# Block sums of the first products' weights: from pass 1 to pass 2

## The chip, the cores and the metric

The kernel runs on one core of a Trainium2 chip. The metric is the device time of one execution, in microseconds; the time of a kernel is the median of its runs.

## The reference

Attention with a compressive memory, followed by two feed-forward networks on the same 2304 tokens (4 batches of 576, model width 512):

```python
def _moe_ref(x, w_gate, w_val, w_out):
    g = x @ w_gate
    silu = g * (1.0 / (1.0 + np.exp(-g)))
    val = x @ w_val
    return (silu * val @ w_out).astype(np.float32)
...
def _moe2_ref(x, w_in, w_out):
    h = x @ w_in
    g = h * (1.0 / (1.0 + np.exp(-1.702 * h)))
    return (g @ w_out).astype(np.float32)
...
    x = np.ascontiguousarray(attn_out.transpose(0, 2, 1, 3)).reshape(B * S, H * D)
    x = _moe_ref(x=x, **moe_kwargs)
    return _moe2_ref(x=x, **moe2_kwargs)
```

The width between is 1536 in the first network (layer one below) and 2048 in the second (layer two). The weights come in 64-bit floats. The products are made to nearly full single precision: an operand is split into a high half, rounded to the type that the matmul reads (fp32r), and a low half, the rest, and a product is high x high + high x low + low x high.

## The kernel before

Activations lie transposed, model width on partitions, tokens on columns. Work goes in two passes over the tokens. Both are laid out by a planner written in the kernel: every step is an entry in `ops` with its engine, an assumed duration, a key (a due time; the lowest key that is ready goes first), what it waits for, and which ring of buffers it takes or gives back. `schedule` plays the entries through and returns one list; `pinned` emits them in that order, with every instruction tied behind the one before it on its engine, so that an engine works in the order of the plan.

Pass 1 takes the first 1024 tokens through both layers with ordinary products (line 89, tile `m`), and makes the attention of all tokens beside that. The weights are 68 chunks of 128 x 512 (`order`), each group of layer one being 8 chunks of its input weights and 4 of its output weights, each group of layer two 4 and 4. A chunk i is loaded by SyncE (`load_w`, L121), decoded to single precision by ScalarE (L140, L141), VectorE (L144, L146, L147) and GpSimd (L150) into a tile `wa`, and split by ScalarE (`spl0`, L161) and GpSimd (`spl1`, L164) into `wp`. There are three `wa`; one is free again when all readers are done.

Pass 2 takes the other 1280 tokens. It uses a scheme of Strassen's kind (Winograd's form) on 2 x 2 blocks: seven products in place of eight, on sums of weight blocks and of activation blocks. A pair of chunks (i even, i + 1) holds four quarters of 128 x 256. Of a pair's seven weight operands two are in the split `wp` (tile `da`), one in another part of `wp` (`dz`), and four are plain sums and differences of the quarters, which have to be split anew. What pass 2 needs is written to DRAM in pass 1 (`keep`, L177 to L187), ten blocks of 256 columns for each pair, in `kept`.

A product whose input is the layer's input is called a first product (`first(i)` is true; `P` in the plan), one whose input is the hidden activations a second product (`Q`). There are 20 pairs of the first kind (12 in layer one, 8 in layer two) and 14 of the second. Before the change the two kinds differ:

- For first products, pass 1 makes the four sums: `add_up` (L170, L171, L174, L175), four GpSimd instructions for each pair into the tile `sums`, after the pair's second chunk is split. They are written to `kept[:, 6:10]` in one transfer.
- For second products, the raw quarters are written (two transfers for each pair), and pass 2 makes the sums in place, by `add` (L1018), four GpSimd instructions for each pair.

In pass 2, SyncE fetches the four blocks (`raw`, L1005; two buffers) once both the last chunk of pass 1 is kept and the buffer is free. ScalarE makes the high half of each (`wh`, L1026), GpSimd the low half (`wl`, L1029), into a ring of six tiles `wb`, and TensorE multiplies (line 89, tile `c`). VectorE evicts and combines products (L1078, L1091, L1151, which read one operand from PSUM, or for L1091 also both from SBUF), makes the sums of activation blocks (L1113, `t1` to `t4`) and most of their low halves (L1134); GpSimd makes some of these low halves (L1134), and the multiplication by the gate (L1095). Two groups are interleaved, and units of layer two's first group two by two.

In the plan, the sums of pass 1 hold a place behind the split (`need + 5.0`), the in-place additions of pass 2 one right ahead of the first split of their quarters (`key - 1.0`).

Of the kernel before, what the change touches and what calls it, by code (L numbers as in the profile page):

```python
# [35 lines left out]
def tile_attention_moe_moe(  # L36
# [75 lines left out]
    def first(i):  # L112
        return layer(i)[1] < layer(i)[2]

    kept = {i: dram.tile([128, 10, 256], F32, name=f"w{i}") for i in range(0, NCK, 2)}
    bits, raws, parts, sums, stages = {}, {}, {}, {}, {}
# [49 lines left out]
    def add_up(i, x):  # L166
        a1, a2 = (raws[n].rearrange("p (a n) -> p a n", a=2) for n in (i - 1, i))
        if x == 0:
            m = sums[i] = d2.tile([128, 4, 256], F32, tag="sums", name="sums", bufs=1)
            nc.gpsimd.tensor_add(m[:, 2], a2[:, 0], a2[:, 1])  # L170
            nc.gpsimd.tensor_sub(m[:, 0], m[:, 2], a1[:, 0])  # L171
        else:
            m = sums[i]
            nc.gpsimd.tensor_sub(m[:, 1], a1[:, 0], a2[:, 0])  # L174
            nc.gpsimd.tensor_sub(m[:, 3], a1[:, 1], m[:, 0])  # L175

    def keep(i):  # L177
        odd, to = i % 2, kept[i - i % 2]
        w = f(parts[i])
        if odd:  # L180
            nc.sync.dma_start(out=to[:, 4:6], in_=w[:, :, 256:512])
        else:
            nc.sync.dma_start(out=to[:, 0:4], in_=w)
        if not first(i):
            nc.sync.dma_start(out=to[:, 6 + 2 * odd:8 + 2 * odd], in_=raws[i].rearrange("p (a n) -> p a n", a=2))
        elif odd:
            nc.sync.dma_start(out=to[:, 6:10], in_=sums.pop(i))  # L187
# [393 lines left out]
    def decode_ops(ops, i, use, split=True, decode=True):  # L581
# [11 lines left out]
        _, at_, ins, _ = layer(i)  # L593
        odd = i % 2
        if at_ >= ins:
            ops["keep", i] = "SP", 0.8 if odd else 1.2, need + 2.0, (("spl1", i),), (), (("wa", ("dec0", i)),)
            return
        if odd:
            for x in range(2):
                ops["sum", i, x] = "Pool", 1.75, need + 5.0, (("spl1", i),) if x == 0 else (("sum", i, 0),), \  # L600
                    ("sums",) if x == 0 else (), tuple(("wa", ("dec0", n)) for n in (i - 1, i)) if x else ()
        ops["keep", i] = "SP", 1.2 if odd else 0.8, need + 6.0, (("sum", i, 1) if odd else ("spl1", i),), (), (
            (("sums", ("sum", i, 0)),) if odd else ())
# [143 lines left out]
    def plan_three(ops, t0, ready, gets):  # L747
# [25 lines left out]
        for m, (i, j) in enumerate(flat):  # L773
            part = "da" if j < 2 else "raw" if j < 6 else "dz"
            key = keys[m] - (WB if part == "raw" else 0.0)
            new = seq[m][0] == "P"
            if (part, i) not in ops:
                ops[part, i] = "SP", 0.55 if part == "dz" else 1.1, key - (RAW if part == "raw" else DIR), (
                    ("seam", 1), *gets), (part,), ()
                if part == "raw" and not new:  # L780
# [546 lines left out]
```

## Time and profile before

| | us |
|---|---|
| median of 3 runs | 1019.97 (1019.64 to 1020.27) |
| the profiled execution | 1020.71 |
| its span, first to last instruction | 1018.9 |
| TensorE busy | 991.2 |
| VectorE busy | 838.0 |
| ScalarE busy | 562.8 |
| GpSimd busy | 696.8 |

The busy time of TensorE is from matmuls whose ends are modelled, so that a busy TensorE may still hide short waits. The granted clock of TensorE was at its full 2.4 GHz in nearly all of the span (mean 0.995). Times in the traces below are counted from the first instruction; pass 1 ends and pass 2 begins near 585 us, and layer two of pass 2 takes over from layer one around 777 to 832 us.

### The profile page before, as it was taken

Reading aid. Unit: us, or ns where it says so; the run is one execution under the profiler, and the core shown is the slowest. Engines: PE = TensorE matmul, PEld = TensorE weight load, DVE = VectorE, ACT = ScalarE, POOL = GpSimd, SP = SyncE. Lnnn points to the kernel's source line nnn. Section 1 sums busy time; section 2 is a strip of 40 time slices with the busy share of each in tenths; the row PEclk is TensorE's granted clock in tenths of the full one; section 3 lists DMA queues with packets and bytes.
Section 4 is the critical chain, followed back from the end, with each engine's and each line's share of the span. In section 5 each row is a group of like instructions: output and inputs, shape, how many; then the busy total and the mean of one; then the engine's idle time right before and its main releaser. Section 6 shows DMA issues by size and latency. Waiting matters only on the chain.

```text
span 1018.9 us, 16779 instructions
## 1 busy us (share of the span) xinstructions
PE 991.2 (97%) x5959; PEld 854.7 (84%) x5959; DVE 838.0 (82%) x1163; ACT 562.8 (55%) x1129; POOL 696.8 (68%) x703
## 2 busy tenths in 40 slices
PE   7998999999999999999999999999999899999997
PEld 4665777777777777777888899999999889999997
DVE  8998589789779889767868957747858999798988
ACT  6887575766465657675645534534324357454541
POOL 7887778997779685856656447748748646756564
PEclk9998999999999999999999999999999999999999
DMA  5353376757547555635575553333333242433322
GB/s 167 109 185 113 118 243 209 248 193 237 210 165 229 206 170 191 222 137 185 186 240 186 206 179 111 100 108 105 114 94 105 83 124 77 132 102 105 111 67 104
DMA packets 63300, 157.34 MB, mean 154 GB/s; under 512 B 8944, under 2 KB 18160, under 8 KB 63216
## 3 DMA queue, kind: packets, MB, share of 16 engines
q1 hardware_dynamic: 63072, 156.26, 46.7%
q8 instruction: 47, 0.77, 0.3%
q14 instruction: 37, 0.30, 0.1%
q10 hardware_dynamic: 144, 0.00, 0.0%
HBM read 104.34 MB, written 51.90 MB: 153 GB/s over the span
## 4 chain that ended last, share of the span: by engine, by line
PE 79%; DVE 17%; issue 1%; DMA 1%; ACT 1%; POOL 0%; SPq 0%; ACTq 0%; DVEq 0%
PE c L89 36%; PE m L89 31%; PE o L89 5%; PE s L89 3%; PE tp L363 2%; DVE nm L312 2%; DVE hl L968 1%; DVE phi L256 1%; DVE s L310 1%; DVE tl L1134 1%; DVE t L1113 1%; DVE acc L1151 1%; DVE wa L146 1%; DVE acc L1113 1%; DVE wa L147 1%
## 5 line engine op out<-in xcount | busy, mean ns | idle before, releaser
L89 PE MATMUL m<-xh,wp 128*128 128x512 f32 x640 | 210.0, 398 | 0.0
L1029 POOL TENSOR_TENSOR wb<-raw,wb 128x256 fp32r<-128x256 f32 x136 | 123.5, 919 | 86.9 <-ACT wb L1026 84.2
L89 PE MATMUL m<-hh,wp 128*128 128x512 f32 x448 | 148.0, 399 | 0.8 <-POOL wp L164 0.7
L89 PEld LDWEIGHTS m<-xh,wp 128*128 128x128 f32 x640 | 120.2, 188 | 32.9 <-issue 5.1
L150 POOL TENSOR_TENSOR wa<-wa,wr 128x512 uint32<-128x512 uint32 x68 | 99.0, 1456 | 62.8 <-DVE wa L147 51.2
L89 PE MATMUL m<-xl,wp 128*128 128x512 f32 x320 | 124.8, 390 | 0.0
L164 POOL TENSOR_TENSOR wp<-wa,wp 128x512 fp32r<-128x512 f32 x68 | 94.9, 1396 | 40.8 <-ACT wp L161 32.4
L1078 DVE TENSOR_TENSOR t<-t,c 128x640 f32<-128x640 f32 x100 | 81.4, 816 | 45.1 <-PE c L89 43.5
L1026 ACT CAST wb<-raw 128x256 fp32r<-128x256 f32 x136 | 53.2, 405 | 108.4 <-PE c L89 95.0
L89 PEld LDWEIGHTS m<-hh,wp 128*128 128x128 f32 x448 | 83.9, 188 | 23.7 <-issue 3.8
L1129 ACT CAST f<-t 128x640 fp32r<-128x640 f32 x98 | 69.4, 726 | 59.4 <-DVE t L1113 32.1
L89 PE MATMUL c<-f,wb 128*128 128x320 f32 x672 | 101.3, 309 | 0.3 <-DVE f L1134 0.3
L89 PEld LDWEIGHTS c<-f,wb 128*128 128x128 f32 x672 | 99.2, 188 | 0.5 <-DVE f L1134 0.5
L351 POOL TENSOR_SCALAR p<-p,sm 128x256 f32<-128x256 f32 (+3 forms) x128 | 78.5, 629 | 19.6 <-DVE sm L343 9.4
L89 PE MATMUL m<-hl,wp 128*128 128x512 f32 x224 | 87.5, 391 | 0.8 <-DVE hl L968 0.8
L1134 DVE TENSOR_TENSOR f<-t,f 128x640 fp32r<-128x640 f32 x70 | 76.5, 1096 | 10.1 <-ACT f L1129 9.8
L326 ACT ACTIVATE p<-s,nm 128x256 f32<-128x256 f32 (+3 forms) x128 | 66.1, 530 | 29.4 <-DVE nm L312 24.4
L1134 POOL TENSOR_TENSOR f<-t,f 128x640 fp32r<-128x640 f32 x28 | 50.4, 1801 | 39.9 <-ACT f L1129 39.8
L1113 DVE TENSOR_TENSOR t<-t,t 128x640 f32<-128x640 f32 x64 | 73.2, 1150 | 1.7 <-POOL t L1095 1.0
L89 PEld LDWEIGHTS m<-xl,wp 128*128 128x128 f32 x320 | 60.2, 188 | 11.6
L161 ACT CAST wp<-wa 128x512 fp32r<-128x512 f32 x68 | 42.3, 621 | 50.0 <-POOL wa L150 19.8
L147 DVE SCALAR_TENSOR_TENSOR wa<-w,wa 128x512 uint32<-128x512 uint32 x68 | 65.7, 965 | 2.3
(138 smaller groups left out, 2422.2 us busy)
## 6 DMA issues: line engine op xcount, KB each, us to landing
w<-w SPq DMA_DIRECT2D x40, 512.0 KB, 3.9
w<-wp SPq DMA_DIRECT2D x34, 512.0 KB, 2.9
raw<-w SPq DMA_DIRECT2D x34, 512.0 KB, 3.6
da<-w SPq DMA_DIRECT2D x34, 512.0 KB, 4.2
w<-wo SPq DMA_DIRECT2D x28, 512.0 KB, 4.0
w<-sums SPq DMA_DIRECT2D x20, 512.0 KB, 2.9
qk<-qk SPq DMA_DIRECT2D x32, 288.0 KB, 3.8
w<-wp SPq DMA_DIRECT2D x34, 256.0 KB, 2.6
```

Source lines behind the costliest of these rows:

```text
L89: nc.tensor.matmul(o, w, x, start=start, stop=stop, skip_group_check=more)
L147: nc.vector.scalar_tensor_tensor(au, top, 0xC0000000, au, op0=ALU.bitwise_and, op1=ALU.bitwise_or)
L150: nc.gpsimd.tensor_tensor(au, au, r, op=ALU.add)
L164: nc.gpsimd.tensor_sub(parts[i][:, 1], raws[i], f(parts[i][:, 0]))
L326: nc.scalar.activation(p[:, j, c:c + n], s[:, j, c:c + n], AF.Exp, bias=nm[:, x, j:j + 1], accum_out=sm[:, x, j:j + 1])
L351: nc.gpsimd.tensor_scalar(p[:, j, c:c + n], p[:, j, c:c + n], sm[:, x, j:j + 1], 1.0, op0=ALU.mult, op1=ALU.mult)
L1026: nc.scalar.copy(wb[:, 0], weight(m))
L1029: nc.gpsimd.tensor_sub(WBS[m][:, 1], weight(m), f(WBS[m][:, 0]))
L1078: nc.vector.tensor_add(wide_(t), wide_(TT[(a, *U)]), pc("P", *U, j))
L1113: nc.vector.tensor_sub(t, block(G, a, kd), block(G, b, kd))
L1129: nc.scalar.copy(form(G, F, kd)[0], block(G, SRC[F], kd))
L1134: e.tensor_sub(l, block(G, SRC[F], kd), f(h))
```

## The change

The sums for first products are no longer made in pass 1. `add_up`, its two entries of the plan for each pair and the tile `sums` go. `keep` writes the raw quarters of every chunk, and every pair's quarters are summed in pass 2 by `add`, as those of second products are: the entries `add` are made for all 34 pairs, `wh` waits for the fourth, and `weight` picks the block in the order that `add` leaves. `keep` has the same place in the plan (`need + 2.0`) for every chunk, and a `wa` is given back by it. `wl`, `raw`, the rings and the keys of all else stay.

```diff
--- before.py
+++ after.py
@@ -109,11 +109,8 @@
     def layer(i):
         return (0, i % 12, 8, i // 12) if i < 36 else (1, (i - 36) % 8, 4, (i - 36) // 8)
 
-    def first(i):
-        return layer(i)[1] < layer(i)[2]
-
     kept = {i: dram.tile([128, 10, 256], F32, name=f"w{i}") for i in range(0, NCK, 2)}
-    bits, raws, parts, sums, stages = {}, {}, {}, {}, {}
+    bits, raws, parts, stages = {}, {}, {}, {}
 
     def load_w(i):
         if wide:
@@ -163,17 +160,6 @@
     def spl1(i):
         nc.gpsimd.tensor_sub(parts[i][:, 1], raws[i], f(parts[i][:, 0]))
 
-    def add_up(i, x):
-        a1, a2 = (raws[n].rearrange("p (a n) -> p a n", a=2) for n in (i - 1, i))
-        if x == 0:
-            m = sums[i] = d2.tile([128, 4, 256], F32, tag="sums", name="sums", bufs=1)
-            nc.gpsimd.tensor_add(m[:, 2], a2[:, 0], a2[:, 1])
-            nc.gpsimd.tensor_sub(m[:, 0], m[:, 2], a1[:, 0])
-        else:
-            m = sums[i]
-            nc.gpsimd.tensor_sub(m[:, 1], a1[:, 0], a2[:, 0])
-            nc.gpsimd.tensor_sub(m[:, 3], a1[:, 1], m[:, 0])
-
     def keep(i):
         odd, to = i % 2, kept[i - i % 2]
         w = f(parts[i])
@@ -181,10 +167,7 @@
             nc.sync.dma_start(out=to[:, 4:6], in_=w[:, :, 256:512])
         else:
             nc.sync.dma_start(out=to[:, 0:4], in_=w)
-        if not first(i):
-            nc.sync.dma_start(out=to[:, 6 + 2 * odd:8 + 2 * odd], in_=raws[i].rearrange("p (a n) -> p a n", a=2))
-        elif odd:
-            nc.sync.dma_start(out=to[:, 6:10], in_=sums.pop(i))
+        nc.sync.dma_start(out=to[:, 6 + 2 * odd:8 + 2 * odd], in_=raws[i].rearrange("p (a n) -> p a n", a=2))
 
     BLOCKS = (((1, 0), (0, 256)), ((2, 0),), ((3, 0),), ())
     NP = B * HP
@@ -590,17 +573,7 @@
             return
         ops["spl0", i] = "Act", 0.63, need, (("dec2", i),), ("wp",), ()
         ops["spl1", i] = "Pool", 1.42, need, (("spl0", i),), (), ()
-        _, at_, ins, _ = layer(i)
-        odd = i % 2
-        if at_ >= ins:
-            ops["keep", i] = "SP", 0.8 if odd else 1.2, need + 2.0, (("spl1", i),), (), (("wa", ("dec0", i)),)
-            return
-        if odd:
-            for x in range(2):
-                ops["sum", i, x] = "Pool", 1.75, need + 5.0, (("spl1", i),) if x == 0 else (("sum", i, 0),), \
-                    ("sums",) if x == 0 else (), tuple(("wa", ("dec0", n)) for n in (i - 1, i)) if x else ()
-        ops["keep", i] = "SP", 1.2 if odd else 0.8, need + 6.0, (("sum", i, 1) if odd else ("spl1", i),), (), (
-            (("sums", ("sum", i, 0)),) if odd else ())
+        ops["keep", i] = "SP", 0.8 if i % 2 else 1.2, need + 2.0, (("spl1", i),), (), (("wa", ("dec0", i)),)
 
     def unit_ops(ops, i, c, key, ends, bank, lead=2.0):
 
@@ -773,16 +746,15 @@
         for m, (i, j) in enumerate(flat):
             part = "da" if j < 2 else "raw" if j < 6 else "dz"
             key = keys[m] - (WB if part == "raw" else 0.0)
-            new = seq[m][0] == "P"
             if (part, i) not in ops:
                 ops[part, i] = "SP", 0.55 if part == "dz" else 1.1, key - (RAW if part == "raw" else DIR), (
                     ("seam", 1), *gets), (part,), ()
-                if part == "raw" and not new:
+                if part == "raw":
                     for x in range(4):
                         ops["add", i, x] = "Pool", 0.7, key - 1.0, (("add", i, x - 1) if x else ("raw", i),), (), ()
             if part == "raw":
                 ops["wh", m] = "Act", 0.32, key, (
-                    ("raw", i) if new else ("add", i, 3), *([("wh", wh)] if wh is not None else [])), ("wb",), ()
+                    ("add", i, 3), *([("wh", wh)] if wh is not None else [])), ("wb",), ()
                 ops["wl", m] = "Pool", 0.7, key, (("wh", m),), (), (("raw", ("raw", i)),) if ends[i, "raw"] == m else ()
                 wh = m
         start = {}
@@ -1019,7 +991,7 @@
 
     def weight(m):
         i, j = flat[m]
-        return RAWS[i][:, j - 2 if first(i) else (0, 2, 3, 1)[j - 2]]
+        return RAWS[i][:, (0, 2, 3, 1)[j - 2]]
 
     def wh(m):
         wb = WBS[m] = cb.tile([128, 2, 256], F32R, tag="wb", name="wb")
@@ -1210,10 +1182,10 @@
     emit = attention(att)
     emit.update(
         w=load_w, dec0=lambda i: dec(i, 0), dec1=lambda i: dec(i, 1), dec2=lambda i: dec(i, 2), spl0=spl0, spl1=spl1,
-        sum=add_up, keep=keep, pe=pe, tanh=tanh, gate=gate1, val=val, hh=hh, hl=hl, acc=acc_in, out=out_to, y_hi=y_hi,
+        keep=keep, pe=pe, tanh=tanh, gate=gate1, val=val, hh=hh, hl=hl, acc=acc_in, out=out_to, y_hi=y_hi,
         y_lo=y_lo)
     for n, size in {"qk": 2, "nq": 2, "v": 2, "qt": 2, "e": 2, "ph": 2, "p": 4, "pt": 1, "st": 1, "zb": 1, "sc": 3,
-                    "big": 3, "wa": 3, "wr": 2, "sums": 1, "wp": 4, "u": 3, "h": 4, "m": 4}.items():
+                    "big": 3, "wa": 3, "wr": 2, "wp": 4, "u": 3, "h": 4, "m": 4}.items():
         at["fifo"][n] = size, []
     at["slots"]["ps"] = [0.0] * 4
     ops = plan_one()
```

## Rows read from the trace of the kernel before

**Rows 1.** Busy time of each engine over the whole span, the page's part 1.

```profile
PE 991.2 (97%) x5959; PEld 854.7 (84%) x5959; DVE 838.0 (82%) x1163; ACT 562.8 (55%) x1129; POOL 696.8 (68%) x703
```

**Rows 2.** By stage: length, then busy us of PE, PEld, DVE, ACT, POOL.

```profile
150.00:200.00 50.00, 47.94 (x248) 35.95 (x247) 43.16 (x62) 31.21 (x63) 44.03 (x41) 1.00 0.72 227
...
200.00:550.00 350.00, 350.00 (x1794) 275.22 (x1793) 282.24 (x420) 211.50 (x423) 251.88 (x243) 1.00 0.59 200
581.00:777.00 196.00, 195.02 (x1321) 194.09 (x1320) 134.36 (x146) 77.01 (x144) 128.17 (x120) 1.00 0.38 121
777.00:832.00 55.00, 48.79 (x319) 46.56 (x318) 54.62 (x64) 26.87 (x48) 30.86 (x26) 1.00 0.34 100
832.00:1010.00 178.00, 177.98 (x1213) 177.98 (x1214) 161.83 (x182) 87.98 (x155) 112.26 (x104) 1.00 0.30 95
```

**Rows 3.** Groups by line, sums of pass 1: busy us, mean ns, idle before.

```profile
L171 POOL TENSOR_TENSOR sums<-sums,wa 128x256 f32<-128x256 f32 x20 | 16.9, 844 | 1.6
L170 POOL TENSOR_TENSOR sums<-wa 128x256 f32<-128x256 f32 x20 | 16.8, 840 | 0.0
...
L174 POOL TENSOR_TENSOR sums<-wa 128x256 f32<-128x256 f32 x20 | 16.2, 812 | 0.0
L175 POOL TENSOR_TENSOR sums<-wa,sums 128x256 f32<-128x256 f32 x20 | 16.2, 811 | 0.0
```

**Rows 4.** Waits, whole span: who waited for whom, us, times, longest.

```profile
ACT wa L140 <- POOL sums L174: 4.5, 2, 2.5
...
ACT wa L140 <- DMA w<-wa: 4.2, 3, 2.5
```

**Rows 5.** Waits from 120 to 205 us.

```profile
PEld m L89 <- POOL wp L164: 1.6, 2, 0.8
```

**Rows 6.** Timeline, VectorE and GpSimd around 158 us: start, us, what.

```profile
156.91 1.78 DVE L147 SCALAR_TENSOR_TENSOR wa<-w,wa 128x512 uint32<-128x512 uint32 x1
...
158.10 1.19 POOL L170 TENSOR_TENSOR sums<-wa 128x256 f32<-128x256 f32 x1
...
161.45 1.75 POOL L150 TENSOR_TENSOR wa<-wa,wr 128x512 uint32<-128x512 uint32 x1
```

**Rows 7.** Tile raw: duration ns min/median/max, first and last start.

```profile
L1018 POOL TENSOR_TENSOR raw<-raw x56: 730/834/1393, 624.6 to 981.0; 128x256 f32<-128x256 f32 x56
...
DMA to landing us min/median/max: 3.3/3.6/6.9
```

**Rows 8.** Timeline, start of pass 2: SyncE, GpSimd, TensorE.

```profile
576.75 0.44 SPq L1005 DMA_DIRECT2D raw<-w  x1
...
581.72 4.68 POOL L1029 TENSOR_TENSOR wb<-raw,wb 128x256 fp32r<-128x256 f32 x4 [7.68 <-ACT wb L1026]
...
586.62 0.46 PE L89 MATMUL c<-th,wb 128*128 128x320 f32 x2
```

**Rows 9.** Timeline, seam of the layers: SyncE, VectorE, GpSimd.

```profile
783.67 8.55 SPq L1005 DMA_DIRECT2D raw<-w  x2
...
792.64 0.81 DVE L1113 TENSOR_TENSOR t<-t,t 128x640 f32<-128x640 f32 x1
...
798.67 1.35 DVE L1113 TENSOR_TENSOR t<-t,t 128x640 f32<-128x640 f32 x1
...
798.00 1.34 POOL L1029 TENSOR_TENSOR wb<-raw,wb 128x256 fp32r<-128x256 f32 x1 [0.84 <-POOL wb L1029]
...
800.91 1.99 POOL L1134 TENSOR_TENSOR f<-t,f 128x640 fp32r<-128x640 f32 x1 [1.57 <-ACT f L1129]
```

**Rows 10.** Groups by line, VectorE's evictions, 787 to 802 us.

```profile
L1151 DVE SCALAR_TENSOR_TENSOR acc<-c,acc 128x640 f32<-128x640 f32 x6 | 4.7, 810 | 0.0
...
L1151 DVE SCALAR_TENSOR_TENSOR csum<-c,csum 128x640 f32<-128x640 f32 x3 | 2.4, 809 | 0.0
```

**Rows 11.** Timeline, VectorE's waits for a product in layer two, first and last.

```profile
881.67 0.82 DVE L1078 TENSOR_TENSOR t<-t,c 128x640 f32<-128x640 f32 x1 [2.76 <-PE c L89]
...
980.21 0.82 DVE L1078 TENSOR_TENSOR t<-t,c 128x640 f32<-128x640 f32 x1 [1.37 <-PE c L89]
```

## The prediction

> **What bounds the kernel now.** The first view is the busy table of the page [rows 1]: TensorE is busy for 97% of the span, VectorE for 82%, GpSimd for 68%. An average like that names TensorE, but the change moves GpSimd work from one half of the kernel to the other, so the second view is the table of busy time by stage [rows 2]. The reader is to look for the stages in which TensorE is not full, since only there can a microsecond be won, and for the engine that is full in its place. From 200 to 550 us (the body of pass 1) TensorE is busy for 350.00 of 350 us. From 150 to 200 us it is busy for 47.94 of 50, and GpSimd, at 44.03, is busier than VectorE. From 581 to 777 us (layer one of pass 2) TensorE has 195.02 of 196. From 777 to 832 us, the seam between the layers of pass 2, it has 48.79 of 55 and VectorE has 54.62: VectorE is the bound there, and 6.2 us of TensorE are lost. From 832 to 1010 us TensorE is full again (177.98 of 178), with VectorE close behind at 161.83. So GpSimd bounds no long stage. It matters where it delays VectorE, and where its place in a chain decides when TensorE gets an operand.
>
> **Removed from pass 1.** 20 pairs of weight chunks lose four GpSimd instructions each, 80 in all; their four groups are busy for 16.8 + 16.9 + 16.2 + 16.2 = 66.1 us [rows 3]. In the 350 full microseconds this is worth nothing: TensorE's own work covers it, and without it GpSimd would idle more. In the stage that is not full it has a price. There the sums of one pair begin at 158.10, the next chunk's last decode instruction follows them at 161.45, while VectorE had finished the step before it at 156.91 + 1.78 = 158.69 [rows 6]. The sums kept that chunk back by 161.45 - 158.69 = 2.8 us. What the chunk feeds is late for TensorE by less: in 120 to 205 us TensorE waited for the split weights 1.6 us in two waits, 0.8 each [rows 5]. At most the whole idle of the stage, 50 - 47.94 = 2.1 us, comes back [rows 2]; at least nothing, because the VectorE steps of the following chunks are then next and are not shortened much. I take -1.0, between one such wait and both.
>
> **Moved in pass 1.** The first products' chunks now go to DRAM as raw quarters, 40 transfers of 256 KB in place of 20 of 512 KB, so bytes stay as they are and SyncE issues 20 more. The buffer of a raw chunk (three of them) was free when the sums had read it; now it is free when the transfer has landed. Twice in the run ScalarE waited for sums to free such a buffer, 4.5 us together, and three times for a transfer of a raw chunk, 4.2 us [rows 4]. The second kind is there today for 28 chunks and will be for 68, so by proportion 4.2 x 68 / 28 = 10.2 us: 6.0 more, against 4.5 less. That net 1.5 us falls on ScalarE, which is 55% busy [rows 1], and what is queued behind the waiting instruction there are the next tanh, split and exponent steps. I cost it at nothing, with +1.5 as its bad end; the good end, the 4.5 alone, lies within the 2.1 already counted.
>
> **Added to pass 2.** Each of the 20 first-product pairs gets four in-place additions on GpSimd between the landing of its quarters and their split. The second products have them today: 56 instructions, at least 0.730, median 0.834, at most 1.393 us [rows 7]. 80 of them are 66.7 us at the median. They fall into four places.
>
> At the start of pass 2 the first quarters are fetched at 576.75 [rows 8] and land some 3.6 us later [rows 7], near 580.4. Four low halves of the split then take 4.68 us, 1.17 each, beside VectorE's work, the first starting at 581.72; the first product that uses one starts at 586.62 [rows 8]. With four additions ahead, at 0.73 to 1.17 each, the first split ends 2.9 to 4.7 us later than 581.72 + 1.17 = 582.9, at 585.8 to 587.6. The cover ends at 586.62, so this costs 0 to 1.0 us. I take +0.4. TensorE is the only one to pay here, and everything after is shifted by it.
>
> In the rest of layer one, 12 pairs make 48 additions, 40.0 us at the median and 66.9 at the slowest. GpSimd is busy for 128.17 of 196 us [rows 2] and would reach 168 to 195. VectorE at 134.36 has room for being slowed. TensorE's cover is the ring of six split blocks. I take 0, with +1.5 as the bad end, since GpSimd works in the order of the plan and the multiplications by the gate stand in the same queue.
>
> At the seam VectorE has no idle time. The quarters for the first two units of layer two are fetched there, by two issues from 783.67 to 792.2 [rows 9], so eight additions run between about 787 and 802, on GpSimd's idle gaps of that stretch. What they cost is what they do to VectorE. A subtraction with both operands in SBUF takes two thirds more beside GpSimd: the one at 792.64, with GpSimd idle, took 0.81 us, the one at 798.67, beside the split that GpSimd began at 798.00, took 1.35 [rows 9]. The difference is 0.54 us. From 787 to 802 us 9 of VectorE's 20 instructions are evictions that read one operand from PSUM [rows 10]; about half have both in SBUF. So 8 x 0.54 / 2 = 2.2 us, at least 0, at most 8 x 0.54 = 4.3. Besides, the GpSimd split at 800.91 [rows 9] feeds a product that TensorE waits for; an addition that starts just before it pushes it by one instruction, 0.73 us, at most two (2 x 1.39). I take 2.2 + 0.7 = +2.9, with 0 and 4.3 + 2.8 = 7.1 as the ends.
>
> The contention is the one place where a rule may be weighed. The Trainium skill, SBUF — State Buffer, sections Who interferes with whom and Summary: rules for kernel authors, says that a VectorE instruction with two SBUF inputs contends with a GpSimd instruction that reads SBUF, and that the second of them to issue is blocked until the first has finished. The rows show a slowing by 0.54 us, less than a whole addition of 0.73; by the rule the seam would cost 8 x 0.73 / 2 = 2.9 instead of 2.2, and the sum below would be 0.7 us higher.
>
> After the seam, 24 additions come in three clusters of eight or fewer. VectorE is 91% busy, but catches up with TensorE once per group of units: at 881.67 it had waited 2.76 us for a product, at 980.21 still 1.37, three such places in all [rows 11]. A cluster slows it by 8 x 0.54 / 2 = 2.2 us, which these waits take up for the most part. I take +0.5 for the whole stage, from 0 to 6 (three clusters with every addition on a two-operand instruction, 3 x (4.3 - 1.37) = 8.8, less what the buffers between VectorE and TensorE hold). Nothing moves at the very end, where no first product is left.
>
> **The sum.** -1.0 + 0.4 + 0 + 2.9 + 0.5 = +2.8 us. It is made against the profiled execution, 1020.71 us with a span of 1018.9; that lies 0.74 above the median of the timed runs, 1019.97. Carried to the median: 1022.8 us, 0.27% slower. About 0.2%, 2.0 us, is what a measurement of this kernel can tell from no change.
>
> **The rivals.** First, no change: the eight additions at the seam meet VectorE mostly while it reads PSUM, and the split at 800.91 keeps its place. Then the seam costs 0.5 instead of 2.9 and the sum is +0.4: 1020.4 us. For it speaks that GpSimd has 55 - 30.86 = 24 us idle in that stage; against it, that the quarters land in the part where its queue is denser.
>
> Second, faster: the stage from 150 to 200 us is bound by the queue of GpSimd more than the waits say. Once the sums are out, the whole 2.1 us idle comes back, and the same again out of waits that the modelled end of a matmul hides, while the additions of pass 2 are free as in the first rival but for the start: -4.2 + 0.4 + 0.5 = -3.3, 1016.7 us. It decides if TensorE's gaps between 140 and 180 us vanish. Against it: TensorE's waits for split weights are 1.6 us there [rows 5], and VectorE's steps, which stay, feed the same chunks.
>
> Third, much slower: after the seam VectorE's slack (1.37 us at the smallest place) is less than what a cluster of eight additions takes from it, so every group of units ends with TensorE waiting, about 2 us in each of three groups on top of the forecast: 1022.8 + 6 - 0.5 = 1028.3 us. For it speaks the 91%; against it, that the catch-up of today is there in every group [rows 11].
>
> **How the numbers follow.** The forecast has 0.47, no change 0.26, faster 0.12, much slower 0.15. The forecast's own range is 1021.0 to 1026 (seam from 1.1 to 6), so that a tenth of its chance counts as no change. Slower by over 0.2%: 0.42 + 0.15 = 0.57; within: 0.26 + 0.05 = 0.31; faster: 0.12. The range that leaves out no more than two in ten reaches from below the first rival into part of the second, and nearly to the third: 1018.4 to 1027.8.
>
> **What would show it.** In the profile after: no group of sums, and 136 additions where 56 were. TensorE still full from 200 to 550 us and its busy time in 150 to 200 us up by about 1 us. The first product on a split block at most 1 us later against the start of pass 2. The seam stretch longer by about 3 us, with VectorE full in it and more of its two-operand instructions near 1.35 than near 0.81. In layer two, TensorE full, and VectorE's waits for products shorter than 2.76 and 1.37, but there. The prediction is wrong if the seam keeps its length, if TensorE shows gaps in layer one, where it now shows none, or if pass 1 ends earlier or later by more than 2 us.

## The result and the profile after

The changed kernel takes 1030.0 us (median of 4 runs, 1028.58 to 1031.18) against 1020.12 for the kernel before beside it (1019.64 to 1021.85): a ratio of 1.0100, with an interval of 1.0088 to 1.0112. Forecast were 1022.8, in a range that ended at 1027.8. The direction was right; the loss is 9.9 us instead of 2.8.

The profiled execution took 1029.59 us, with a span of 1027.8. The busy table of the page (engine, busy us, share of the span, instructions) beside [rows 1]:

```profile
PE 991.1 (96%) x5959; PEld 856.0 (83%) x5959; DVE 838.5 (82%) x1163; ACT 562.6 (55%) x1129; POOL 706.2 (69%) x703
```

TensorE and VectorE did the same work as before; GpSimd has 9 us more. The four groups of [rows 3], 66.1 us, are gone, and the additions of pass 2 are now 136, with a mean of 0.992 us (the 56 of [rows 7] had a median of 0.834):

```profile
L990 POOL TENSOR_TENSOR raw<-raw 128x256 f32<-128x256 f32 x136 | 134.7, 992 | 14.9 <-DMA raw<-w 7.3
```

By stage, to be laid beside [rows 2] (bounds of a stretch, its length, then busy us of PE, PEld, DVE, ACT and POOL, granted clock, DMA share, GB/s; the bounds of pass 2 are moved by the 4 us that it starts later):

```profile
150.00:200.00 50.00, 48.81 (x253) 37.60 (x254) 47.34 (x69) 36.59 (x75) 41.34 (x36) 1.00 0.75 253
200.00:550.00 350.00, 348.99 (x1789) 273.95 (x1788) 264.41 (x418) 209.66 (x418) 197.75 (x181) 1.00 0.59 197
585.00:781.00 196.00, 195.02 (x1320) 194.05 (x1319) 138.94 (x145) 74.84 (x139) 161.81 (x160) 1.00 0.34 109
781.00:840.00 59.00, 50.48 (x321) 47.91 (x319) 58.64 (x63) 25.92 (x45) 40.12 (x35) 0.97 0.31 94
840.00:1018.00 178.00, 177.96 (x1213) 177.96 (x1214) 166.71 (x182) 88.07 (x157) 137.32 (x128) 1.00 0.29 95
```

Where the time went is seen best by cutting the span at the same matmuls in every trace. There are 1632 of tile `m` (pass 1) and 2856 of tile `c` (pass 2), in the same order in each kernel. The cuts are the starts of `m` 1 and 97 and of `c` 1, 169, 1345 and 1513 (the first product of layer two's own weights), and the end of the last `c`. Each column is the us from one cut to the next; the experiments stand here too.

| kernel | to `m` 1 | to `m` 97 | to `c` 1 | to `c` 169 | to `c` 1345 | to `c` 1513: the seam | last `c` | span's end |
|---|---|---|---|---|---|---|---|---|
| before | 99.58 | 38.14 | 447.12 | 25.87 | 172.41 | 29.57 | 200.84 | 5.35 |
| after | 97.70 | 44.54 | 446.85 | 25.87 | 172.41 | 33.34 | 200.83 | 6.26 |
| pass 1 alone | 98.96 | 45.73 | 446.60 | 25.87 | 172.41 | 29.56 | 200.85 | 5.88 |
| pass 2 alone | 99.94 | 38.29 | 446.60 | 26.47 | 172.41 | 33.31 | 201.41 | 6.36 |
| gate | 100.33 | 39.10 | 447.08 | 25.87 | 172.41 | 33.99 | 200.70 | 6.28 |
| no additions at the seam | 99.83 | 44.53 | 446.59 | 25.87 | 172.41 | 29.57 | 200.83 | 6.54 |
| half | 100.81 | 43.70 | 446.32 | 25.87 | 172.41 | 31.44 | 200.83 | 6.30 |
| twice | 100.52 | 43.84 | 446.80 | 25.87 | 172.41 | 41.19 | 200.82 | 6.26 |
| fills at the seam | 99.17 | 44.22 | 446.62 | 25.87 | 172.41 | 30.27 | 200.84 | 6.27 |
| order of before, no sums | 98.77 | 38.20 | 447.36 | 26.35 | 172.41 | 33.33 | 200.83 | 6.27 |
| order of before, sums of 36 and 38 | 98.95 | 38.28 | 446.71 | 26.20 | 172.41 | 29.56 | 200.83 | 6.17 |

The 8.9 us between the two profiled spans lie in three places: +6.4 from `m` 1 to `m` 97, the first 40 us in which pass 1 multiplies; +3.8 at the seam; +0.9 behind the last product. The first column took -1.9 back, but it varies from 97.7 to 100.8 among the six kernels that have the changed pass 1 as it is. The other columns of the two agree within 0.3 us; the same pass 1 takes 447.12 and 446.60 us up to `c` 1 in two traces (before, pass 2 alone), so half a microsecond there tells nothing. At the first place, the larger, the prediction had put nothing.

**What happens there.** Chunks 3 and 4 now decode in the middle of the last attention head. In the kernel before, ScalarE began on chunk 3 at 107.70, behind the sums of chunks 0 and 1 on GpSimd and the exponents of that head, and VectorE followed at 108.42 (start us, us, instruction):

```profile
103.92 0.72 POOL L170 TENSOR_TENSOR sums<-wa 128x256 f32<-128x256 f32 x1
107.70 0.69 ACT L140 ACTIVATE wa<-w 128x512 f32<-128x512 f32 x1
108.42 0.83 DVE L144 TENSOR_SCALAR wa<-wa 128x512 f32<-128x512 f32 x1
```

In the changed kernel ScalarE begins on chunk 3 at 93.89 and on chunk 4 at 101.94, and VectorE's three steps for each stand between the maxima (L295) and sums (L325) of the attention head that TensorE waits for:

```profile
93.89 0.70 ACT L137 ACTIVATE wa<-w 128x512 f32<-128x512 f32 x1
101.94 0.66 ACT L137 ACTIVATE wa<-w 128x512 f32<-128x512 f32 x1
96.35 0.72 DVE L141 TENSOR_SCALAR wa<-wa 128x512 f32<-128x512 f32 x1
97.11 0.80 DVE L143 TENSOR_SCALAR wa<-wa 128x512 uint32<-128x512 uint32 x1
97.94 1.06 DVE L144 SCALAR_TENSOR_TENSOR wa<-w,wa 128x512 uint32<-128x512 uint32 x1
98.92 1.23 DVE L325 SCALAR_TENSOR_TENSOR sm<-sm,ilt 128x1 f32<-128x1 f32 x1
104.08 1.23 DVE L295 TENSOR_REDUCE nm<-s 128x2 f32<-128x1024 f32 x1
105.22 0.44 DVE L141 TENSOR_SCALAR wa<-wa 128x512 f32<-128x512 f32 x1
105.40 0.69 ACT L309 ACTIVATE p<-s,nm 128x512 f32<-128x512 f32 x1 [0.63 <-DVE nm L295]
104.38 0.63 PE L350 MATMUL tp<-ident,p 128*128 128x128 f32 x4 [1.78 <-POOL p L334]
106.94 1.26 PE L265 MATMUL tphi<-ident,phi 128*128 128x128 f32 x5 [1.82 <-ACT p L309]
```

The last two lines are TensorE's waits: 1.78 us for the exponents that GpSimd normalises, and 1.82 us until ScalarE was done with the raw ones. From 88 to 108 us VectorE is busy for 19.23 us, before for 15.22: it has become the bound of that stretch (columns as in the stage table; before, then changed):

```profile
88.00:108.00 20.00, 19.49 (x144) 12.85 (x142) 15.22 (x36) 16.63 (x49) 15.72 (x21) 0.95 0.26 95
```

```profile
88.00:108.00 20.00, 15.69 (x111) 10.90 (x110) 19.23 (x36) 16.40 (x46) 16.84 (x21) 0.98 0.37 132
```

The plan made the change: a chunk takes one of the three `wa`, and `wa` of chunks 0 and 1 were held until their sums (the first at 103.92 in the trace of before); now `keep` gives them back after the split, and the planner, which takes whatever is ready with the lowest key, moves the next chunks forward.

TensorE also pays a second time for idling, by its clock (stretch, length, busy us, granted clock, DMA share, GB/s). First the kernel before, then the changed kernel, then the run of pass 1 alone:

```profile
104.00:108.00 4.00, 3.96 (x41) 1.00 0.09 35
```

```profile
100.00:104.00 4.00, 2.60 (x13) 1.00 0.50 197
104.00:108.00 4.00, 1.79 (x11) 0.88 0.07 25
108.00:112.00 4.00, 4.00 (x33) 0.70 0.30 109
```

```profile
104.00:108.00 4.00, 0.74 (x5) 0.93 0.06 23
108.00:112.00 4.00, 3.79 (x13) 0.50 0.37 133
112.00:116.00 4.00, 4.00 (x43) 0.71 0.00 0
```

In the last, after 4 us with 0.74 us of work, the engine ran at 0.50, the lower of its two levels (1.2 GHz), for 4 us. So the +6.4 of the changed kernel is made of idle time, 8 - 2.60 - 1.79 = 3.6; the clock, 4 x 0.12 + 4 x 0.30 = 1.7; and one more wait of 0.8 for VectorE at 129 us: 6.1. In pass 1 alone it is 3.6 + 3.4 + 0.8 = 7.8, measured +7.6.

### The profile page after: what moved, and what is told of

Its sections match the earlier page's. It is cut to its first block, busy times and chain, and to the rows that moved or that the text cites. A ratio compares the mean times of both kernels' runs of the same rounds, so it can differ in the third digit from the quotient of the medians.

```text
span 1027.8 us, 16840 instructions
## 1 busy us (share of the span) xinstructions
PE 991.1 (96%) x5959; PEld 856.0 (83%) x5959; DVE 838.5 (82%) x1163; ACT 562.6 (55%) x1129; POOL 706.2 (69%) x703
## 4 chain that ended last, share of the span: by engine, by line
PE 75%; DVE 17%; issue 2%; ACT 2%; DMA 2%; POOL 1%; SPq 1%; ACTq 0%; DVEq 0%; POOLq 0%
PE c L89 35%; PE m L89 30%; PE o L89 4%; PE s L89 3%; PE tp L346 2%; DVE nm L295 2%; DVE t L1085 1%; DVE acc L1123 1%; DVE f L1106 1%; ACT p L309 1%; DVE s L293 1%; DVE wa L144 1%; DVE acc L1128 1%; DVE wa L141 1%; DVE sm L325 1%
## 5 line engine op out<-in xcount | busy, mean ns | idle before, releaser
L990 POOL TENSOR_TENSOR raw<-raw 128x256 f32<-128x256 f32 x136 | 134.7, 992 | 14.9 <-DMA raw<-w 7.3
L147 POOL TENSOR_TENSOR wa<-wa,wr 128x512 uint32<-128x512 uint32 x68 | 96.6, 1422 | 63.5 <-DVE wa L144 20.9
L998 ACT CAST wb<-raw 128x256 fp32r<-128x256 f32 x136 | 51.0, 404 | 84.7 <-PE c L89 59.0
L1106 DVE TENSOR_TENSOR f<-t,f 128x640 fp32r<-128x640 f32 x70 | 84.4, 1208 | 9.4 <-ACT f L1101 9.3
L309 ACT ACTIVATE p<-s,nm 128x256 f32<-128x256 f32 (+3 forms) x128 | 66.1, 532 | 25.3 <-DVE nm L295 21.6
L1085 DVE TENSOR_TENSOR t<-t,t 128x640 f32<-128x640 f32 x64 | 78.3, 1232 | 1.1
L1106 POOL TENSOR_TENSOR f<-t,f 128x640 fp32r<-128x640 f32 x28 | 47.9, 1710 | 31.4 <-ACT f L1101 28.2
L89 PE MATMUL c<-xh,wb 128*128 128x320 f32 x320 | 66.4, 310 | 1.0 <-DVE t L1050 1.0
```

Source lines behind the costliest of these rows:

```text
L89: nc.tensor.matmul(o, w, x, start=start, stop=stop, skip_group_check=more)
L147: nc.gpsimd.tensor_tensor(au, au, r, op=ALU.add)
L309: nc.scalar.activation(p[:, j, c:c + n], s[:, j, c:c + n], AF.Exp, bias=nm[:, x, j:j + 1], accum_out=sm[:, x, j:j + 1])
L990: nc.gpsimd.tensor_tensor(t[:, to], t[:, a], t[:, b], op=op)
L998: nc.scalar.copy(wb[:, 0], weight(m))
L1085: nc.vector.tensor_sub(t, block(G, a, kd), block(G, b, kd))
```

## The experiments

The first four were to separate the two places and to test the cause of each.

**Pass 1 alone.** Pass 1 as changed; pass 2 without additions for first products:

```diff
-                if part == "raw":
+                if part == "raw" and not first(i):
...
-                    ("add", i, 3), *([("wh", wh)] ...
+                    ("raw", i) if first(i) else ("add", i, 3), *([("wh", wh)] ...
```

> Pass 1 as changed (no sums, raw quarters kept), pass 2 as before: no additions for first products, which take the raw quarters as they lie; so the sums of the first products are left out of the computation. Theory (the loss has two places: the order of pass 1 costs 4.2 us between the first product of pass 1 and the first of pass 2, the seam of pass 2 the rest): the first product of pass 2 starts at about 589 us, the seam is as before, and the median is 1024 us (1023 to 1025). Rival (pass 1 differs only by a shift that pass 2 would swallow, and all of the loss is the additions in pass 2): 1020 us.

Measured: 1027.46 us, ratio 1.0068 (1.0053 to 1.0083). The seam is as before to 0.01 us, and pass 1 alone loses 7.0 us, more than the 4.2 expected. That 4.2 was the difference of two start times in single traces, of which the changed kernel's had reached `m` 1 by 1.9 us sooner; cut at `m` 1 it would have been 6.1. The clock covers the rest: it cost 3.4 us in this run and 1.7 in the changed kernel, as worked out above.

**Pass 2 alone.** Pass 1 of the kernel before, with its sums, and additions for all pairs:

```diff
-                if part == "raw" and not new:
+                if part == "raw":
...
-                    ("raw", i) if new else ("add", i, 3), *([("wh", wh)] ...
+                    ("add", i, 3), *([("wh", wh)] ...
```

> Pass 1 as before (sums made and kept), pass 2 as changed: four additions on GpSimd for every pair of chunks, so that the pairs of first products get their additions on top of sums and their weights are other than the reference's. Theory of two places: the first product of pass 2 starts at about 585 us as before, the first product P(1,0) of the second layer's own weights is 3.7 us later, some 0.9 us more at the tail: median 1024.7 us (1023.5 to 1026). Rival (the seam is late only because pass 1 ended late or another way round): 1020 us. Rival (the additions cost more when they are not hidden behind a late pass 1): 1028 us or more.

Measured: 1025.19 us, ratio 1.0045 (1.0028 to 1.0061): +4.7, as the theory of two places has it. The seam takes 33.31 us, 3.74 more than before, and `c` 1 starts at 584.83 us (before 584.85). Two smaller losses show here that the changed kernel does not have: 0.60 us at the start of pass 2 and 0.57 between the seam and the last product. The two runs together lose 11.7 us, the changed kernel 9.9; these two and the longer drop of the clock in pass 1 alone cover the difference.

**Gate.** The changed kernel, with chunks 3 and 4 tied behind the exponents of the last head:

```diff
-            ops["dec0", i] = "Act", 1.38, need - 4.0, (("w", i),), ("wa", "wr"), ()
+            late = (("expo", 7, 3),) if i in (3, 4) else ()
+            ops["dec0", i] = "Act", 1.38, need - 4.0, (("w", i), *late), ("wa", "wr"), ()
```

> The changed kernel with one more condition: the decoding of chunks 3 and 4 waits, as it in effect did in the kernel before, until the last attention head's exponentials are issued. Theory (the release of the staging buffers by an earlier transfer lets chunks 3 and 4 decode in the middle of the last attention head, and that makes the gaps of TensorE at 104 to 107 us): those gaps shrink to under 1 us each, the first product of pass 2 starts at about 585 us, and the median is 1026 us (1025 to 1027). Rival (pass 1 is late because of the transfers of quarters themselves or the freed GpSimd time, whatever the order): 1029 to 1031 us.

Measured: 1026.78 us, ratio 1.0067 (1.0047 to 1.0087). The gaps are gone, and so is the clock's drop (same columns as above):

```profile
104.00:108.00 4.00, 3.97 (x32) 1.00 0.05 17
108.00:112.00 4.00, 4.00 (x49) 1.00 0.01 2
```

From `m` 1 to `m` 97 it takes 39.10 us instead of 44.54. The order of two chunks is thus the cause of 5.4 of the 6.4 us; the wait of 0.8 that comes later (here at 126 us) stays. Against the expectation the start of pass 2, at 586.5 us, is 1.5 late, half of it in the first column, and the seam has 0.65 more than in the changed kernel. The trace shows where: TensorE starts on the seam's last products 31.49 us behind its beginning (31.47 in the changed kernel), but its granted clock falls to 0.50 at 817.4, in the middle of them. By the medians this kernel is 3 us faster than the changed one and not 5.4, since in its trace the first column and the seam take 2.6 and 0.65 back.

**No additions at the seam.** The changed kernel without the sums of pairs 36 and 38:

```diff
-                if part == "raw":
+                if part == "raw" and i not in (36, 38):
```

> The changed kernel without the additions for the pairs 36 and 38, the two whose additions fall at the start of layer two; the sums of those two pairs are left out. Theory (the eight GpSimd additions at the seam, by their own time and by what they do to VectorE's two-operand instructions beside them): the first product of layer two's own weights comes 3.7 us earlier relative to the start of pass 2 than in the changed kernel, the median is 1026.3 us (1025.5 to 1027.5). Rival (the seam is late by the order that the planner chose after pass 1, not by the additions there): 1029 to 1031 us.

Measured: 1027.06 us, ratio 1.0066 (1.0051 to 1.0081), and a seam of 29.57 us, the same as before to 0.01. The whole loss at the seam comes from these eight additions; the order that the planner chose elsewhere plays no part.

What about them costs 3.77 us was still open. In the trace they stand in GpSimd's queue ahead of the two splits that TensorE waits for (start us, us, instruction; compare 794.29 in the trace of before and 800.91 in [rows 9]):

```profile
796.08 4.57 POOL L990 TENSOR_TENSOR raw<-raw 128x256 f32<-128x256 f32 x4
800.61 1.57 POOL L1106 TENSOR_TENSOR f<-t,f 128x640 fp32r<-128x640 f32 x1
802.83 5.32 POOL L990 TENSOR_TENSOR raw<-raw 128x256 f32<-128x256 f32 x4
809.39 1.52 POOL L1106 TENSOR_TENSOR f<-t,f 128x640 fp32r<-128x640 f32 x1
```

That looks like a queue. VectorE in the same stretch looks like contention (start us, us, instruction): beside the additions seven of its two-operand instructions take 1.35 us or so and one 0.81. Against the same instructions in the trace of before, five gained 0.55 us each, one 0.40 (it took 0.97) and one nothing (it took 1.35 already); 0.66 more is on an `acc` instruction behind the additions, 1.99 us instead of 1.33, which meets GpSimd's work otherwise than before. That makes 3.8 us.

```profile
796.14 1.36 DVE L1106 TENSOR_TENSOR f<-t,f 128x640 fp32r<-128x640 f32 x1
797.42 2.64 DVE L1085 TENSOR_TENSOR t<-t,t 128x640 f32<-128x640 f32 x2
802.18 1.37 DVE L1106 TENSOR_TENSOR f<-t,f 128x640 fp32r<-128x640 f32 x1
803.47 1.35 DVE L1106 TENSOR_TENSOR xl<-acc,xh 128x640 fp32r<-128x640 f32 x1
805.49 0.81 DVE L1106 TENSOR_TENSOR f<-t,f 128x640 fp32r<-128x640 f32 x1
806.22 1.35 DVE L1085 TENSOR_TENSOR t<-t,t 128x640 f32<-128x640 f32 x1
807.49 1.35 DVE L1106 TENSOR_TENSOR xl<-acc,xh 128x640 fp32r<-128x640 f32 x1
```

Two runs tell the theories apart, by the number of additions.

**Half.** Two of the four additions for each of the two pairs:

```diff
-                    for x in range(4):
+                    for x in range(2 if i in (36, 38) else 4):
```

> The changed kernel with two of the four additions for each of the pairs 36 and 38 (four in place of eight at the seam); half of the sums of those two pairs are left out. Measured as the interval from the first product of pass 2 to the first product of layer two's own weights: 227.8 us before, 231.6 to 232.3 with eight additions, 227.8 with none. Queue theory (the GpSimd splits that TensorE waits for stand behind the additions in GpSimd's queue, and the delay is what does not fit into GpSimd's idle time there; two additions take some 2.4 us, its idle time ahead of each split was 2.4 and 2.8 us): 227.8 to 228.5 us. Contention theory (each addition lengthens VectorE's two-operand instructions beside it, and the sum of that is the delay, so half the additions cost half): 229.7 to 230 us. The median goes with it: 1027 or 1028.5 us.

**Twice.** Each of the eight additions issued two times:

```diff
-        nc.gpsimd.tensor_tensor(t[:, to], t[:, a], t[:, b], op=op)
+        for _ in range(2 if i in (36, 38) else 1):
+            nc.gpsimd.tensor_tensor(t[:, to], t[:, a], t[:, b], op=op)
```

> The changed kernel with each of the eight additions for pairs 36 and 38 made twice in a row, so that the weights of these two pairs are other than the reference's. Queue theory (GpSimd has no idle time left at the seam, so each further addition of 1.2 us is paid in full): the interval from the first product of pass 2 to the first of layer two's own weights grows by 8 x 1.2 = 9.6 us, to 241 us (239 to 243), and the median to 1037 to 1040 us. Contention theory (only the lengthened VectorE instructions count): it grows by as much again as the first eight cost, 3.8 us or less, to 235.4 us, median 1033 us.

Measured: 1029.67 us for half and 1038.18 for twice (ratios 1.0093, 1.0077 to 1.0108, and 1.0177, 1.0161 to 1.0194). The seam's excess over before is 0 with no additions, 1.87 us with four, 3.77 with eight, 11.62 with sixteen. Up to eight it is contention: 0.47 us for each on average, and it equals what VectorE's 20 instructions TENSOR_TENSOR of the seam take more in sum (20.7 us before, 22.6 with four, 24.5 with eight), while VectorE is idle for 0.24 us of the seam in all three. With eight, TensorE's granted clock also falls (a mean of 0.95 over the seam; 1.00 before and with four). That can't be a second cause: VectorE never waited for TensorE there. GpSimd was not what half waited for: its splits stood waiting for the high half from ScalarE, 3.1 us in two waits (before 4.0). From eight to sixteen it is the queue: +7.85 us for 16.6 - 9.4 = 7.2 us of additions (9.4 for the eight of the changed kernel); the remaining 0.7 falls behind the second pushed split, where from 820.2 to 826.2 us TensorE works at a granted clock of 0.50. VectorE now waits for TensorE, and TensorE for the splits on GpSimd. The groups of VectorE's evictions and of the additions in the seam of that run (busy us, mean ns, idle us before and what ended it), and TensorE's waits:

```profile
L1124 DVE SCALAR_TENSOR_TENSOR acc<-c,acc 128x640 f32<-128x640 f32 x9 | 7.1, 816 | 9.2 <-PE c L89 9.2
L991 POOL TENSOR_TENSOR raw<-raw 128x256 f32<-128x256 f32 x16 | 16.6, 1035 | 1.1
PE c L89 <- POOL f L1107: 9.2, 2, 5.2
```

So each theory holds on one side of a point, and the changed kernel stands on VectorE's side, close to it. The median of half is 1.2 us above the higher of its two expectations; in its trace the first column is 3.1 us longer than the changed kernel's, which hides the 1.9 us that it has less at the seam. Twice grew by less than the 9.6 us expected, since an addition takes 1.04 us there, where VectorE often waits, and not 1.18.

**Fills at the seam.** Two constant fills in place of each addition, to see what part of an addition VectorE feels:

```diff
-        nc.gpsimd.tensor_tensor(t[:, to], t[:, a], t[:, b], op=op)
+        if i in (36, 38):
+            for _ in range(2):
+                nc.gpsimd.memset(t[:, to], 1.0)
+        else:
+            nc.gpsimd.tensor_tensor(t[:, to], t[:, a], t[:, b], op=op)
```

> The changed kernel with each of the eight additions for pairs 36 and 38 replaced by two GpSimd fills with a constant of the same 128x256 block, which write but read nothing; the sums of those two pairs are left out. It tells what about an addition lengthens VectorE's two-operand instructions. If it is GpSimd's reading of SBUF, the seam interval falls back to 227.8 to 228.3 us and VectorE's instructions there keep a mean near 1.09 us. If any GpSimd instruction with SBUF as its target does it, in proportion to its time, the interval is 229.5 us or more, with VectorE's two-operand instructions near 1.2 us. Median 1026 to 1027.5, or 1028 us and more.

Measured: a seam of 30.27 us, 0.70 more than before; the median is 1028.36 (1.0073, 1.0051 to 1.0096). It lies between the two expectations, near the first: with 16 fills of about 0.3 us, 4.6 us in all, VectorE's TENSOR_TENSOR instructions take 0.65 us more, a seventh of GpSimd's added time, against 3.8 / 9.4, two fifths, for the additions. In this stretch the means of VectorE's groups `t`, `xl` and `csum` are those of before; `f` and `acc` alone are longer. In the trace these are two instructions. An `f` at 801.55 us, 1.30 us instead of 0.97, stands beside a split and a fill; an `acc` at 807.84, 1.62 instead of 1.33, stands beside GpSimd instructions that read, and beside no fill. The four that stand beside fills alone (from 797.06, two from 797.79, from 802.78) keep 0.81 us. So a fill by itself slowed nothing, and 0.29 of the 0.65 us comes from instructions that the fills have moved; whether the fill has a part in the `f`'s 0.33 is open. The Trainium skill, SBUF — State Buffer, section Who interferes with whom, says that a VectorE instruction with two SBUF inputs contends with a GpSimd instruction that reads SBUF and not with one that only writes it; the four that kept 0.81 us beside fills agree.

**Order of before, no sums.** Was the gain of pass 1, for which the forecast had -1.0, there at all? Pass 1 in the order of before, with the place of the sums kept in the plan and nothing issued for it; pass 2 as changed:

```diff
+    def summed(i):
+        return i - i % 2 in ()
...
     def add_up(i, x):
+        if not summed(i):
+            return
...
-        if not first(i):
+        if not summed(i):
             nc.sync.dma_start(out=to[:, 6 + 2 * odd:8 + 2 * odd], in_=raws[i] ...
```

> Pass 1 in the order of the kernel before (its plan still reserves the time of the sums on GpSimd and holds the staging buffers until then), but no sum is made and the raw quarters are kept; pass 2 as changed. Theory (the order of chunks 3 and 4 is what pass 1 lost; the absent sums themselves give time back, as forecast): the first product of pass 2 starts at 582 to 584 us against 584.9 before and 589 to 591 in the changed kernel; the seam interval is 231.6 to 232.3 us as changed; median 1023.5 us (1022 to 1024.5). Rival (the transfers of the quarters or their time are what pass 1 lost): first product of pass 2 at 587 us or later, median 1027 us or more.

Measured: 1025.47 us, ratio 1.0056 (1.0039 to 1.0072). That is 2 us above what was expected. `c` 1 starts at 584.3 us in the trace, but counted from `m` 1 this is 38.20 + 447.36 = 485.56 us, against 485.26 before. With the order of before, then, pass 1 loses nothing and gains nothing, and the transfers of raw quarters cost nothing. From 165 to 185 us TensorE is busy for 18.25 us instead of 17.94: 0.3 us came back. Two waits for GpSimd at 242.6 us, 0.9 and 0.2, took it again, and the start of pass 2 costs 0.5.

**Order of before, sums of 36 and 38.** The same, but these two pairs keep their sums in pass 1, so that nothing is added at the seam: the version to which the other runs point.

```diff
+    def summed(i):
+        return i - i % 2 in (36, 38)
...
     def add_up(i, x):
+        if not summed(i):
+            return
...
-                if part == "raw" and not new:
+                if part == "raw" and not summed(i):
```

> As the run before, but the sums of pairs 36 and 38 alone are made and kept in pass 1 as in the kernel before, so that no additions fall at the seam; all other first products get theirs in pass 2. Theory: first product of pass 2 at 582 to 584.5 us, seam interval 227.8 us, median 1019 us (1018 to 1020), at or a little below the kernel before. Rival (pass 1 gives nothing back, or the additions in the rest of pass 2 cost too): 1021 us or more.

Measured: 1022.41 us (ten runs, 1020.57 to 1024.44), ratio 1.0022 (1.0009 to 1.0035). That is 7.6 us less than the changed kernel, but no gain on the kernel before: the 1019 us expected was missed, and the rival's "1021 us or more" fits. Its profiled execution, 1020.93 us, is among its fastest, and cut by cut that trace is the one of before: 29.56 at the seam, 0.3 more at the start of pass 2, 0.8 behind the last product. Its ten executions differ in TensorE's granted clock: the four at 0.997 or 0.998 took 1020.6 to 1022.2 us, the six at 0.994 or 0.995 1022.2 to 1024.4. Why more of them had the lower one than this trace shows is open.

## Why the prediction was wrong

**The step that failed: "Moved in pass 1".** It said that a raw buffer was free when the sums had read it and is free now when the transfer has landed, weighed 4.5 us of one kind of wait against a proportion of another, found a net 1.5 us on ScalarE and costed it at nothing, with +1.5 as the bad end. It asked only whether buffers would come free later. The waits that it priced stayed small (ScalarE waited 5.6 us for transfers of a raw chunk, in six waits; 10.2 were reckoned). The buffers came free earlier, at the one place where the sums had held them longest, and the planner filled the time with work for the engine that bounds the last attention head. That costs 6.4 us from `m` 1 to `m` 97 in the changed kernel, 5.6 to 7.6 in the five other runs with that pass 1, and the gate takes 5.4 of it back. The trace of before could have warned: the first sums stood at 103.92 with two chunks right behind them, at 107.70 and 108.89, and from 88 to 108 us VectorE was busy for 15.22 of 20 us. Two chunks of 0.83 + 0.69 + 1.05 = 2.57 us on VectorE, moved into that, make 20.4. But the stage table began at 150 us [rows 2]. The marks named in the prediction caught it: it is wrong "if pass 1 ends earlier or later by more than 2 us", and pass 1 ended 4.2 later.

**"Removed from pass 1", -1.0: nothing.** The place was right: its idle time fell (18.25 against 17.94 busy in 165 to 185 us with the order of before; 48.81 against 47.94 in 150 to 200 in the changed kernel, where the same work comes some 4 us later). The sum was not, since new waits of like size came later (1.1 us at 242 there; 1.0 at 427 and 0.9 at 569 in the changed kernel, both absent before). From `m` 97 to `c` 1 the changed kernel is 0.27 us faster in all, less than the 0.5 by which that column varies.

**The start of pass 2, +0.4: right in size, hidden in the changed kernel.** There pass 1 was so late that the first quarters had been added from 575.63 on, 13 us ahead of `c` 1. Where pass 1 is on time, the first additions end 4.63 us after 580.05, and TensorE waits for the split (in the last experiment; start us, us, instruction, idle time before it):

```profile
580.05 4.63 POOL L1022 TENSOR_TENSOR raw<-raw 128x256 f32<-128x256 f32 x4 [7.02 <-DMA raw<-w]
586.95 0.56 PE L89 MATMUL c<-th,wb 128*128 128x320 f32 x2 [1.09 <-ACT wb L1030]
```

That stretch is longer there by 0.33, 0.48 and 0.60 us in the three runs that have it.

**The rest of layer one, 0: right.** 172.41 us in every kernel. GpSimd is at 161.81 of 196 us, against a forecast of 168 to 195; eight of the 48 additions ran before that stretch, from 575.63 us on.

**The seam, +2.9: +3.77, within its ends of 0 and 7.1.** The term was 8 x 0.54 / 2 = 2.2 for contention and 0.7 for a split that is pushed. The first was too small, the second did not occur as a term of its own. The 0.54 us was right (0.81 against 1.35), but the half was not. It came from counting VectorE's instructions from 787 to 802 us, 9 evictions in 20. Work that meets contention stretches and so takes more of the time, and the additions stretch with it (1.18 us each here, by the group of this line in the seam, 0.73 alone): beside them stand eight two-operand instructions, of which seven are slowed, six of them by more than before. Measured for each addition: 0.47 us instead of 0.27, of which 0.08 is the later `acc`. The rule that was weighed there (the Trainium skill, SBUF — State Buffer, section Summary: rules for kernel authors), that the second to issue is blocked until the first has finished, would have given 2.9 for contention, nearer to 3.77, but not for its reason: the slowed instruction still takes 1.36 us and not 0.81 + 0.73, and the additions are slowed as well.

**After the seam, +0.5: nothing up to the last product, +0.7 behind it.** 200.83 us against 200.84. VectorE's slack did take up the additions, as argued, but it was nearly used up. In layer two its waits for a product (total us, times, longest us) shrank; at the places of the first and the last of [rows 11], 2.76 and 1.37 there, they are 0.45 and 0.24:

```profile
DVE t L1050 <- PE c L89: 6.3, 11, 0.9
```

In pass 2 alone the slack did not last: VectorE waits for no product behind 988 us, and TensorE loses 0.57 us before the last one. So the argument held by a narrow margin; what decides between the two was not followed up.

**"Nothing moves at the very end": wrong.** VectorE's last instruction ends 2.95 us behind the last product, and 2.27 in the kernel before. It is 2.94 to 3.29 in all nine kernels with additions in layer two, and 2.27 again in pass 1 alone, which has none. The chain that ended last runs on VectorE without a gap for 13.5 us there, before for 5.8. So the additions after the seam cost 0.7 us in all, near the +0.5, but at the place that was held safe. The other 0.2 of the 0.9 lies behind VectorE's last instruction, in a remainder that varies from 3.1 to 3.6 us among the kernels; it is longest in pass 1 alone, which makes up the +0.5 there.

**The rivals.** None of the three came. "No change" put the seam at 0.5; "faster" wanted 4.2 us from pass 1, and even with the sums out and the old order there was nothing. "Much slower", 1028.3, is near in time and wrong in its mechanism: layer two loses nothing up to its last product. The rival that was missing is an earlier release.

## What to carry to other kernels

When a change takes away a reader of a ring buffer, ask what the earlier release lets start, on which engine, and whether that engine is the bound just there; an order that was good only because a buffer was held should be written down as a condition. Read the stage table from the first microsecond, not from the stage that the change aims at. A contention estimate goes by which instructions stand beside each other once both are stretched, in a stage where the slowed engine has no idle time; and past some number of additions the other engine's queue takes over, which only a run with more of them shows.

## What the runs showed of the hardware

GpSimd's additions and VectorE's instructions with two operands in SBUF slow each other: 0.73 to 1.18 us on the one side, 0.81 to 1.35 on the other, while VectorE's evictions from PSUM beside the same additions keep 0.81. Four of VectorE's two-operand instructions beside fills on GpSimd alone kept 0.81 us. TensorE's clock fell to 0.50 for 4 us after 4 us with 0.74 us of work, and was back at 1.00 some 8 us later; that cost 3.4 us on top of 3.6 us of idle time. In the seam of the changed kernel the clock fell too, and cost nothing, since VectorE was the bound.
